# An order's book-keeping learns of twelve stores and 36 loads that GpSimd issues

## The chip, the cores and the metric

The kernel runs on one core of one Trainium2 chip. The metric is the device time of one execution in microseconds (us). Engine names: TensorE (PE, matmuls), VectorE (DVE), ScalarE (ACT), GpSimd (POOL) and SyncE (SP). DMAs are issued by instructions of SyncE, of ScalarE or of GpSimd; each of these engines takes its instructions in the order in which they were written.

## The reference, cut to what matters

```python
x = A_u                                   # 1 x 2048 x 576, f32
xn = layernorm(x)
# S4D: a long convolution per channel, 576 channels, 128 complex poles each
A = -exp(log_A_real) + 1j * A_imag;  C = (C_real + 1j * C_imag) * dt[:, None]
P = exp((A * dt[:, None])[:, :, None] * arange(2048))
K = 2 * einsum("dn,dnl->dl", C, P).real
s = irfft(rfft(xn, 4096) * rfft(K, 4096))[:2048] + xn * D_skip
# channel MLP, 576 -> 4608 -> 576
h = gelu(layernorm(xn) @ w1 + b1)
g = silu(h @ w2 + b2)
out = x + s * g
```

## The kernel before, in words

The MLP is the bulk. Tokens are held in two blocks of 512 at a time, hidden channels in twelve groups of three blocks of 128. One pair of a group and a token block is a slot; there are 48, and each has three positions of the first layer (`layer1`, 14 matmuls each, L546) and eight of the second (L638, L630, in a few slots L608). Values are split into a high and a low part, so a product takes three matmuls. After a block of the first layer ScalarE computes the gelu (L578) and its high part `hh` (L581), VectorE the low part `hl` (L584), and the second layer reads both. Weights come by SyncE and are split by ScalarE (L530) and VectorE (L527).

Between the positions lies the convolution. The channels are worked in 36 tables of 16 and six chunks of 96. A table takes the poles' parameters of its channels from `par_s` in HBM (`load_par`, L882, GpSimd's queue, two buffers `par`), computes phases (L900, L903, VectorE), folds and sines (L906 to L919, ScalarE) and magnitudes `mg` (L925), weighs them (`U`, `v`, L936 to L942), and TensorE sums over the poles (`kgen`, L982). A chunk transforms input and kernel (L1054, L1093), multiplies, transforms back (L1146, L1178); ScalarE then copies the result out of PSUM into two scratch tiles, one of `pr` and one of `ys` (L1186, two copies), and GpSimd's queue stores each with four DMAs into `s_s` in HBM (L1189). Near the end `combine_load` (L707) and `last_s` (L733) read `s_s` again, for the products with the gate and the output.

Other things on GpSimd's queue: the first layernorms (L414), reordering of constants (L288 to L310), half of `place_rest` (L664, eight small DMAs between SBUF tiles, the other half on SyncE), stores of gates (L685) and of half of the output (L719).

All of this is put into one fixed order by a planner, the class `Order`, while the program is written out. It keeps a clock for each engine. Work is held in lines of steps; a step names an engine, a duration, marks of other steps that it needs, and a mark of its own. A step with an engine starts at the later of its needs and the engine's free time and moves that engine's clock on by its duration; its result counts 0.2 us later (`LAT`). A step without an engine (`None`) writes its instructions as soon as its needs are there and gives its mark the duration later; it moves no engine's clock. Of the steps that can start by TensorE's present time, the one with the earliest start is written first; between equal starts the line that stands earlier in `od.lines` goes first. Urgent chains (gelu, `hl`, additions into `acc`, `place_rest`) have dates by which they must be done, and a line's step that would run past the next such date on its engine is put off.

So the planner's durations decide only the order in which each engine gets its instructions. On the device each instruction waits for its semaphores and for those ahead of it on its engine. In the kernel before, `load_par` is a step without an engine, and the stores L1189 are written inside the ScalarE step that copies (`store`); the planner's clock of GpSimd knows of neither. `place_rest`'s half on GpSimd is a step of 5.2 us.

Of the kernel before, what the change touches and what calls it, by code (L numbers as in the profile page):

```python
# [22 lines left out]
CH = 96  # L23
NCH = D // CH
# [9 lines left out]
PK = 72  # L34
# [9 lines left out]
def dve(n):  # L44
    return 0.075 + 0.00104 * n


def act(n):
    return 0.06 + 0.00098 * n
# [159 lines left out]
def step(eng, dur, fn, need=(), mark=None, cv=0, at=0.0, late=0.0, tbl=None, by=1e9):  # L209
    return dict(eng=eng, dur=dur, fn=fn, need=tuple(need), mark=mark, cv=cv, at=at, late=late, tbl=tbl, by=by)  # L210
# [3 lines left out]
def mixer_kernel(ctx, tc, u, log_a_real, a_imag, c_real, c_imag, log_dt, d_skip, w1, b1, w2, b2,  # L214
# [662 lines left out]
    def load_par(b):  # L877
        if b == NB:
            return
        PAR[b] = sb.tile([P, SB, NPAR], F32, name="par", bufs=2)  # L880

        nc.gpsimd.dma_start(PAR[b].rearrange("p (g i) k -> p g (i k)", g=4), dram(  # L882
            par_s, (b // 6 * CH + b % 6 * 4) * NPAR, [[D * NPAR, P], [24 * NPAR, 4], [1, 4 * NPAR]]))
# [7 lines left out]
    def tables(b):  # L891

        T = {}

        def phase(k):
            if k == 0:
                T["w"] = sb.tile([P, 2, SB, NV], F32, name="w", bufs=2)
                nc.vector.tensor_mul(T["w"][:, 1], bc(PAR[b][:, :, 0], 2, NV), bc(tv, 1, SB))  # L900
            else:
                u = T["w"][:, 1, :, 32:]
                nc.vector.tensor_add(u, u, bc(PAR[b][:, :, 1], 2, 32))  # L903

        def whole():
            nc.scalar.activation(T["w"][:, 0].bitcast(I32), T["w"][:, 1], AF.Copy)  # L906

        def frac():
            nc.vector.tensor_sub(T["w"][:, 1], T["w"][:, 1], T["w"][:, 0].bitcast(I32))

        def fold():
            nc.scalar.activation(T["w"][:, 0], T["w"][:, 1], AF.Abs)

        def sin(k):
            w = T["w"][:, k]
            if k == 0:
                nc.scalar.activation(w, w, AF.Sin, bias=halfpi[:, 0:1], scale=-TWO_PI)
            else:
                nc.scalar.activation(w, w, AF.Sin, scale=TWO_PI)  # L919

        def mags(k):
            if k == 0:
                T["m"] = sb.tile([P, SB, NM], F32, name="mg")
            n, e1, e8 = ((8, E1, E8), (4, E32, E256))[k]
            nc.vector.tensor_mul(T["m"][:, :, 64 * k:64 * k + 8 * n].rearrange("p c (i j) -> p c i j", i=n),  # L925
                                 bc(PAR[b][:, :, e8:e8 + n], 3, 8), bc(PAR[b][:, :, e1:e1 + 8], 2, n))

        def weigh(k, part):

            if part == 0:  # L930
                T["v"] = sb.tile([P, 2, SB, 64], F32, name="v")
                T["U"] = sb.tile([P, 2, SB, 32], F32, name="U")
                TAB[b] = (T["U"], T["v"])
            w, v, m = T["w"], T["v"], T["m"]
            if part == 0:
                nc.vector.tensor_mul(T["U"], w[:, :, :, 32:], bc(m[:, :, 64:], 1, 2))  # L936
            elif part == 1:
                nc.vector.tensor_mul(v[:, :, :, :32], w[:, :, :, :32], bc(m[:, :, :32], 1, 2))
            elif k == 0:
                nc.vector.tensor_mul(v[:, k, :, 32:], w[:, k, :, 31::-1], m[:, :, 32:64])  # L940
            else:
                nc.vector.scalar_tensor_tensor(v[:, k, :, 32:], w[:, k, :, 31::-1], -1.0, m[:, :, 32:64],  # L942
                                               op0=OP.mult, op1=OP.mult)

        n = SB * 32
        f = lambda g, *a: lambda: g(*a)
        return ([step(None, 6.0 if b < 3 else 4.5, lambda: load_par(b), mark=("par", b), need=[("pack", ((b // 6 + 1) * CH - 1) // PK)]
                      + ([("mags", b - 2)] if b > 1 else [("xn", k) for k in range(8, NT)])),
                 step("DVE", dve(SB * NV), f(phase, 0), need=[("wu", b - 2, 1)] if b > 1 else []),
                 step("DVE", dve(n), f(phase, 1)), step("ACT", act(SB * NV), whole),  # L950
                 step("DVE", dve(SB * NV), frac), step("ACT", act(SB * NV), fold, mark=("fold", b))],
                [step("ACT", act(SB * NV), f(sin, 0), need=[("fold", b)], mark=("sin", b, 0), tbl="sin"),
                 step("ACT", act(SB * NV), f(sin, 1), mark=("sin", b, 1), tbl="sin")],
                [step("DVE", dve(2 * n), f(mags, 0), need=[("par", b)]),
                 step("DVE", dve(n), f(mags, 1), mark=("mags", b))]
                + [step("DVE", dve(2 * n) if part < 2 else dve(n), f(weigh, k, part),
                        need=[("sin", b, int(part < 2))] + ([("kg", b - 1)] if b else []),
                        mark=("wu", b, 1) if k else None) for k, part in ((0, 0), (0, 1), (0, 2), (1, 2))])
# [55 lines left out]
    def chunk(c):  # L1014

        XC, MAT, YS = {}, {}, {}
        one, two, three = [], [], []
        line = [one]
        add = lambda *a, **k: line[0].append(step(*a, **k))

# [144 lines left out]
        def i1():  # L1165
            Q = []

            def mm():
                for f in range(2):
                    q = bank2("cv")  # L1170
                    Q.append(q[:, :, :4 * CH].rearrange("p t (i r d) -> p t i r d", i=2, r=2))
                lead(q)
                for t in range(2):
                    for e in range(4):
                        for f in range(2):
                            r = slice(64 * f, 64 * f + 64)
                            k = 4 * e + 2 * t
                            nc.tensor.matmul(Q[f][32 * e:32 * e + 32, t], g1t[r],  # L1178
                                             A2[r, k:k + 2, 1].rearrange("p i d r -> p i r d"),
                                             start=True, stop=True, skip_group_check=True)  # L1180
            add("PE", I1, mm, cv=2, mark=("i1", c))

            def store(f):
                sc = ys_tile().rearrange("p i a b d -> p i (a b) d") if f else (
                    sb.tile([P, 2, 4 * CH], F32, name="pr").rearrange("p t (i d) -> p t i d", i=4))
                nc.scalar.activation(sc, Q[f].rearrange("p t i r d -> p t (i r) d"), AF.Copy)  # L1186
                for e in (1, 3, 0, 2):
                    y, h = divmod(e, 2)
                    nc.gpsimd.dma_start(s_s[64 * y + 32 * f:64 * y + 32 * f + 32, 8 * h:8 * h + 8, c * CH:(c + 1) * CH],  # L1189
                                        sc[32 * e:32 * e + 32].rearrange("p t i d -> p (t i) d"))  # L1190
            for f in range(2):
                add("ACT", act(8 * CH), lambda f=f: store(f), cv=-1, mark=("st", c) if f else None)

        for g in range(4):
            for f in range(2):
                add(None, 4.5 if g == 3 and f == 1 else 1.0, lambda g=g, f=f: load(g, f),
                    need=() if g or f else [("xn", b) for b in range(NT)] + [("pack", D // PK - 1)])
# [15 lines left out]
    od = Order(tc, nc)  # L1213
    od.pinned = True
    el, wl2, wl, nl2, pl, pl2, pl3, pl4, pl5, nl, ml, ml2, xl, wx, c3, c2, c1, kl, tl, sl, vl, gl, fl, f2l = [od.line() for _ in range(24)]
    nlh, mlh, yl, pl6 = od.line(), od.line(), od.line(), od.line()
    od.lines = od.lines[-4:] + od.lines[:-4]
    el2 = od.line()


# [273 lines left out]
    for k in range(4):  # L1494
        gl["steps"].append(step("POOL", 5.0, lambda k=k: part.update({k: load_g2(k)}), mark=("g2", k),
                                need=[("g2c", k - 1)] if k else []))
# [24 lines left out]
    def end_line():  # L1521
        for c, c0, c1, sets in ((NCH - 3, 0, CE, [(b, 1) for b in range(8)]), (NCH - 2, CE, CL, [(0, 4), (4, 4)])):
            for b, n in sets:
                a = (b, n, c0, c1)
                ml["steps"].append(step(None, 8.0 if b else 12.0, lambda a=a: combine_load(*a), need=[("st", c), ("u", NT - 1)]))
                ml["steps"].append(step("DVE", 2 * dve(n * (c1 - c0)), lambda a=a: (gated(*a), summed(*a))))
                ml["steps"].append(step(None, 4.0, lambda: None))
        a = (0, 8, CL, D)
        ml["steps"].append(step(None, 1.0, lambda: combine_load(*a, 0), need=[("k1", NCH - 1, 1), ("x1", NCH - 1)]))
        ml["steps"].append(step(None, 16.0, lambda: combine_load(*a, 1), need=[("st", NCH - 1)]))  # L1530
        ml["steps"].append(step("DVE", dve(8 * CH) + 0.1, lambda: gated(*a)))
        ml["steps"].append(step("DVE", dve(8 * CH) + 0.1, lambda: summed(*a)))

# [36 lines left out]
    later(mid - 4, G - 1, lambda: x_free(0))  # L1570
    later(mid - 1, G - 1, lambda: x_free(1))
    later(NSLOT - 10, 4, end_line)
    sl["steps"].append(step(None, 14.0, last_s, need=[("st", NCH - 1)], mark="s8"))
    for k in range(8):
        c3["steps"].append(step(None, 5.0 if k == 0 else 2.0, lambda k=k: last_x(k), need=[("i1", NCH - 1), ("u", NT - 1)], mark=("x8", k)))

# [198 lines left out]
```

## Time and profile before

| what | us |
|---|---|
| median of 3 runs | 1071.47 (1070.90 to 1071.89) |
| profiled execution, its own time | 1071.01 |
| its span in the profile | 1069.2 |
| TensorE busy | 1058.5 (99%) |
| VectorE busy | 936.8 (88%) |
| ScalarE busy | 683.0 (64%) |
| GpSimd busy | 228.4 (21%) |

A row of the timeline reads: start, us, engine, line, operation, output tile <- input tiles, count, and in brackets the idle time of the engine before it with what released it. A row of waits reads: engine, tile and line, what it waited for, us in total, times, the longest. A row of stretches gives busy us and instruction counts of TensorE, its weight loads, VectorE, ScalarE and GpSimd, then the granted TensorE clock (1.00 is full), the DMA engines' share and GB/s. A row of groups gives us in total and mean ns of one, then the idle time before the group and what ended it. A DMA issue of GpSimd counts as busy time while GpSimd issues it; the landing is listed apart.

### The profile page before, as it was taken

Reading aid. Unit: us, or ns where it says so; the run is one execution under the profiler, and the core shown is the slowest. Engines: PE = TensorE matmul, PEld = TensorE weight load, DVE = VectorE, ACT = ScalarE, POOL = GpSimd, SP = SyncE. Lnnn points to the kernel's source line nnn. Section 1 sums busy time; section 2 is a strip of 40 time slices with the busy share of each in tenths; the row PEclk is TensorE's granted clock in tenths of the full one; section 3 lists DMA queues with packets and bytes.
Section 4 is the critical chain, followed back from the end, with each engine's and each line's share of the span. In section 5 each row is a group of like instructions: output and inputs, shape, how many; then the busy total and the mean of one; then the engine's idle time right before and its main releaser. Section 6 shows DMA issues by size and latency. Waiting matters only on the chain.

```text
span 1069.2 us, 23544 instructions
## 1 busy us (share of the span) xinstructions
PE 1058.5 (99%) x9515; PEld 874.5 (82%) x9515; DVE 936.8 (88%) x1550; ACT 683.0 (64%) x1061; POOL 228.4 (21%) x328
## 2 busy tenths in 40 slices
PE   9999999999999999999999999999999999999997
PEld 7888888888878886888877888878887888778886
DVE  7698768899899897999988989999999999867766
ACT  6658639786755766757686666856785757524344
POOL 5668533201000003002120000200002022242130
PEclk9999999999999999999999999999999999999999
DMA  7785436663213243356422215222421346365146
GB/s 232 239 267 181 123 130 226 231 158 118 92 39 101 50 85 97 98 142 162 92 69 61 92 48 115 67 79 64 106 90 50 122 122 147 101 196 155 48 119 186
DMA packets 145470, 130.93 MB, mean 122 GB/s; under 512 B 94925, under 2 KB 117233, under 8 KB 144337
## 3 DMA queue, kind: packets, MB, share of 16 engines
q1 hardware_dynamic: 127696, 78.77, 27.0%
q0 software_dynamic: 16912, 49.68, 15.0%
q8 instruction: 75, 1.23, 0.5%
q10 hardware_dynamic: 752, 0.97, 0.3%
q14 instruction: 35, 0.28, 0.1%
HBM read 98.90 MB, written 35.19 MB: 125 GB/s over the span
## 4 chain that ended last, share of the span: by engine, by line
PE 95%; DVE 2%; DMA 1%; POOL 1%; issue 1%; ACT 0%; SPq 0%; ACTq 0%; DVEq 0%; POOLq 0%
PE m L546 42%; PE m L638 30%; PE m L630 8%; PE cv L1093 3%; PE cv L982 3%; PE m L608 3%; PE cv L1054 2%; PE cv L1146 2%; PE cv L1178 1%; PE m L561 1%; DMA acc<-in_A_u_dram 0%; PE cv L608 0%; POOL s_s L1189 0%; POOL acc L664 0%; DMA row<-y_s 0%
## 5 line engine op out<-in xcount | busy, mean ns | idle before, releaser
L638 PE MATMUL m<-w2s,hh 128*128 128x448 f32 x1056 | 303.8, 369 | 0.7 <-DVE acc L643 0.6
L578 ACT ACTIVATE h<-m,b1t 128x512 f32<-128x512 f32 x144 | 99.2, 689 | 203.7 <-PE m L546 200.0
L638 PEld LDWEIGHTS m<-w2s,hh 128*128 128x128 f32 x1056 | 194.0, 188 | 36.8 <-issue 12.4
L638 PE MATMUL m<-w2s,hl 128*128 128x448 f32 x528 | 192.0, 364 | 1.8 <-DVE hl L584 1.8
L546 PE MATMUL m<-XH,w1h 128*128 128x512 f32 x564 | 155.2, 397 | 0.0
L546 PE MATMUL m<-XL,w1h 128*128 128x512 f32 x564 | 151.4, 390 | 0.0
L546 PE MATMUL m<-XH,w1l 128*128 128x512 f32 x564 | 151.0, 389 | 0.0
L584 DVE TENSOR_TENSOR hl<-h,hh 128x512 fp32r<-128x512 f32 x144 | 99.8, 694 | 50.6 <-ACT hh L581 50.0
L546 PEld LDWEIGHTS m<-XH,w1h 128*128 128x128 f32 x564 | 103.4, 188 | 30.6 <-issue 5.5
L882 POOL DMA_DIRECT2D par<-par_s x36 | 27.5, 764 | 469.3 <-DVE mg L925 436.7
L546 PEld LDWEIGHTS m<-XL,w1h 128*128 128x128 f32 x564 | 105.9, 188 | 23.0
L546 PEld LDWEIGHTS m<-XH,w1l 128*128 128x128 f32 x564 | 105.9, 188 | 22.5
L643 DVE TENSOR_TENSOR acc<-m,acc 128x448 f32<-128x448 f32 x160 | 98.1, 613 | 22.6 <-PE m L638 21.8
L638 PEld LDWEIGHTS m<-w2s,hl 128*128 128x128 f32 x528 | 99.1, 188 | 9.2 <-DVE hl L584 2.2
L581 ACT ACTIVATE hh<-h 128x512 fp32r<-128x512 f32 x144 | 90.7, 630 | 3.4
L630 PE MATMUL m<-hh,w2s 128*128 128x512 f32 x264 | 90.2, 396 | 0.0
L530 ACT ACTIVATE w2s<-raw 128x576 fp32r<-128x576 f32 (+3 forms) x75 | 46.3, 675 | 36.9 <-PE m L638 35.3
L925 DVE TENSOR_TENSOR mg<-par 128x1024 f32<-128x1024 f32 x72 | 68.0, 951 | 0.8
L630 PEld LDWEIGHTS m<-hh,w2s 128*128 128x128 f32 x264 | 50.3, 190 | 9.9
L527 DVE TENSOR_TENSOR w1l<-raw,w1h 128x384 fp32r<-128x384 f32 x98 | 49.8, 555 | 9.7 <-ACT w1h L530 9.6
L906 ACT ACTIVATE w<-w 128x1024 int32<-128x1024 f32 x36 | 37.9, 1054 | 28.8 <-DVE w L903 28.6
L546 PE MATMUL m<-XR,w1r 128*128 128x512 f32 x141 | 54.8, 389 | 0.0
(229 smaller groups left out, 1901.2 us busy)
## 6 DMA issues: line engine op xcount, KB each, us to landing
raw<-in_B_w_dram SPq DMA_DIRECT2D x75, 288.0 KB, 3.4
raw<-in_B_w_dram SPq DMA_DIRECT2D x100, 192.0 KB, 3.0
par_s<-A POOLq DMA_DIRECT2D x8, 1080.0 KB, 5.6
par<-par_s POOLq DMA_DIRECT2D x36, 240.0 KB, 3.2
f2t<-f2q SPq DMA_DIRECT2D x24, 256.0 KB, 3.7
raw<-in_B_w_dram SPq DMA_DIRECT2D x50, 96.0 KB, 3.4
u_s<-in_A_u_dram POOLq DMA_DIRECT2D x16, 288.0 KB, 4.2
xc<-xn_s SPq DMA_DIRECT2D x48, 96.0 KB, 3.7
```

The lines of the kernel that those rows point to most:

```text
L527: low_on.tensor_sub(lo, r[:m], h[:m].bitcast(F32))
L530: nc.scalar.activation(h, r, AF.Copy)
L546: nc.tensor.matmul(q, a, b, start=j == 0, stop=j == len(ops) - 1)
L578: nc.scalar.activation(t, q, AF.Gelu_apprx_tanh, bias=b1t[:, g * G + i:g * G + i + 1], scale=1.0)
L581: LAST[0] = nc.scalar.activation(hh[:, i], t, AF.Copy)
L584: nc.vector.tensor_sub(hl[:, i], t, hh[:, i].bitcast(F32))
L608: nc.tensor.matmul(q[:, :288], a[:, i, j * P:j * P + P], b[:, i, dh * 288:dh * 288 + 288], skip_group_check=alone, start=i == 0 and k == 0 ...
L630: nc.tensor.matmul(q, a[:, i], b[:, i], start=first and i == 0 and k == 0, stop=slot in CONV and i == G - 1 and k == 2, skip_group_check=True)
L638: nc.tensor.matmul(q[:, :DA], a[:, i, key * P:key * P + P], b[:, i], start=i == 0 and k == 0, stop=i == G - 1 and k == 2)
L643: nc.vector.tensor_add(o, Q2.pop(key)[:, :DA], bias2[:, :DA] if first else o)
L906: nc.scalar.activation(T["w"][:, 0].bitcast(I32), T["w"][:, 1], AF.Copy)
L925: nc.vector.tensor_mul(T["m"][:, :, 64 * k:64 * k + 8 * n].rearrange("p c (i j) -> p c i j", i=n), bc(PAR[b][:, :, e8:e8 + n], 3, 8), bc(P ...
```

## The change

The load of a table's parameters becomes a step of GpSimd of 0.8 us, and a step without an engine behind it stands for the rest of the transfer (5.2 us for the first three tables, 3.7 after; 6.0 and 4.5 in one before). The four DMAs that store a scratch tile leave the copy's step and become a step of GpSimd of their own, 2.4 us, in a new line `zl` that stands behind nearly all others; it needs the copy, and the mark `("st", c)`, on which the reads of `s_s` depend, is now that of the second store's step. The two steps that stand for the last chunk's reads of `s_s` are shortened by 5 us. No instruction is added or removed; what changes is when the planner writes them, and through its clock of GpSimd and its marks the order of the rest.

```diff
-        return ([step(None, 6.0 if b < 3 else 4.5, lambda: load_par(b), mark=("par", b), need=[("pack", ((b // 6 + 1) * CH - 1) // PK)]
+        return ([step("POOL", 0.8, lambda: load_par(b), need=[("pack", ((b // 6 + 1) * CH - 1) // PK)]
                       + ([("mags", b - 2)] if b > 1 else [("xn", k) for k in range(8, NT)])),
+                 step(None, 5.2 if b < 3 else 3.7, lambda: None, mark=("par", b)),
...
+        send_line = zl["steps"]
...
                 nc.scalar.activation(sc, Q[f].rearrange("p t i r d -> p t (i r) d"), AF.Copy)
+                SC[f] = sc
+
+            def send(f):
                 for e in (1, 3, 0, 2):
                     y, h = divmod(e, 2)
                     nc.gpsimd.dma_start(s_s[64 * y + 32 * f:64 * y + 32 * f + 32, 8 * h:8 * h + 8, c * CH:(c + 1) * CH],
-                                        sc[32 * e:32 * e + 32].rearrange("p t i d -> p (t i) d"))
+                                        SC[f][32 * e:32 * e + 32].rearrange("p t i d -> p (t i) d"))
+            SC = {}
             for f in range(2):
-                add("ACT", act(8 * CH), lambda f=f: store(f), cv=-1, mark=("st", c) if f else None)
+                add("ACT", act(8 * CH), lambda f=f: store(f), cv=-1, mark=("sc", c, f))
+                send_line.append(step("POOL", 2.4, lambda f=f: send(f), need=[("sc", c, f)], mark=("st", c) if f else None))
...
+    zl = od.line()
     el2 = od.line()
...
-        ml["steps"].append(step(None, 16.0, lambda: combine_load(*a, 1), need=[("st", NCH - 1)]))
+        ml["steps"].append(step(None, 11.0, lambda: combine_load(*a, 1), need=[("st", NCH - 1)]))
...
-    sl["steps"].append(step(None, 14.0, last_s, need=[("st", NCH - 1)], mark="s8"))
+    sl["steps"].append(step(None, 9.0, last_s, need=[("st", NCH - 1)], mark="s8"))
```

## The prediction

> **What bounds the kernel now.** I read the page first, then a table of equal stretches, then the waits of TensorE, and last the timelines of the one stretch that differs. The page's first rows say that TensorE works all the time:
>
> ```profile
> span 1069.2 us, 23544 instructions
> PE 1058.5 (99%) x9515; PEld 874.5 (82%) x9515; DVE 936.8 (88%) x1550; ACT 683.0 (64%) x1061; POOL 228.4 (21%) x328
> ...
> DVE  7698768899899897999988989999999999867766
> ```
>
> The change removes no matmul, so only TensorE's lost time can be won: 1069.2 − 1058.5 = 10.7 us of idle time, and time at a lower clock. The table in stretches of 27 us (columns: busy us and instructions of TensorE, its weight loads, VectorE, ScalarE, GpSimd; then granted clock, DMA share, GB/s) has one bad row between the start and the last 16 us:
>
> ```profile
> 378.00:405.00 27.00, 27.00 (x271) 21.58 (x277) 26.34 (x40) 18.86 (x28) 4.66 (x8) 1.00 0.35 86
> 405.00:432.00 27.00, 24.63 (x199) 18.58 (x184) 20.82 (x36) 16.51 (x23) 6.63 (x12) 0.94 0.26 71
> 432.00:459.00 27.00, 27.00 (x278) 23.14 (x277) 25.56 (x48) 20.89 (x35) 2.94 (x5) 1.00 0.49 135
> ```
>
> In 405 to 432 TensorE idles 27.00 − 24.63 = 2.37 us, the clock falls, and VectorE, busy 95 to 98% on either side, is over 5 us short. The waits of TensorE, whole span, name the same place:
>
> ```profile
> PE m L638 <- DVE hl L584: 1.8, 1, 1.8
> PE m L1241 <- POOL XL L1232: 1.3, 1, 1.3
> PE cv L432 <- DVE row L405: 0.6, 1, 0.6
> PE m L638 <- DVE acc L643: 0.6, 1, 0.6
> ```
>
> The second and third lie in the first microseconds, which the planner does not order. So before the tail there is one stall, and the first and fourth row are its two halves. Its cause stands in the timelines of GpSimd and VectorE:
>
> ```profile
> 401.09 2.33 POOL L1189 DMA_DIRECT2D s_s<-pr  x4 [16.64 <-ACT pr L1186]
> 403.42 4.38 POOL L664 DMA_DIRECT2D acc<-bias  x8
> 407.79 2.32 POOL L1189 DMA_DIRECT2D s_s<-ys  x4
> 411.31 0.77 POOL L882 DMA_DIRECT2D par<-par_s  x1 [1.19 <-issue]
> ```
> ```profile
> 398.21 0.68 DVE L925 TENSOR_TENSOR mg<-par 128x512 f32<-128x512 f32 x1
> ...
> 407.80 0.65 DVE L584 TENSOR_TENSOR hl<-h,hh 128x512 fp32r<-128x512 f32 x1
> 414.48 1.22 DVE L900 TENSOR_TENSOR w<-par,tv 128x1024 f32<-128x1024 f32 x1 [6.03 <-DMA par<-par_s]
> 415.73 0.69 DVE L903 TENSOR_TENSOR w<-w,par 128x512 f32<-128x512 f32 x1
> 416.34 0.68 DVE L584 TENSOR_TENSOR hl<-h,hh 128x512 fp32r<-128x512 f32 x1
> ```
>
> The next poles' buffer is free when `mg` is read, at 398.89. Their load (L882) goes out at 411.31, because two stores of the convolution's results (L1189) and GpSimd's half of `place_rest` (L664) stand ahead of it. VectorE takes its instructions in order: it sits 6.03 us before L900, and the hidden block's low half (`hl`, L584), which TensorE needs, stands behind L900 and L903. The planner charged GpSimd for none of the eight stores and not for the load, so it believed the parameters there and put L900 first.
>
> **What the stall costs.**
>
> ```profile
> 417.10:421.00 3.90, 3.90 (x10) 3.11 (x11) 3.90 (x7) 3.90 (x10) 0.76 (x1) 0.56 0.21 63
> ```
>
> This is the stretch right after the gap: clock 0.56 over 3.90 us, so 3.90 × 0.44 = 1.72 us lost. Sum: 2.37 idle + 1.72 clock = 4.1 us. Lower bound 2.4, were the slow clock no consequence of the gap; upper bound 4.4, if some 0.3 us of restart at the two halves is added as an estimate.
>
> Here a rule of the Trainium skill says otherwise. "TensorE: Matmul & The Clock Gate", in the part on the HAM clock gate, has the array fall to half clock after at least one idle window of about 3.4 us. The gap before the slow stretch is 1.8 us by the wait row, half of that, and yet the clock halves right behind it; the trace therefore does not agree as far as the length goes. By the page's length the slow clock would not be the gap's doing, and the sum would be 2.4 us; by the rows it is 4.1 us. I take the rows.
>
> **The change, part by part.**
>
> (1) The load of the parameters becomes a step of GpSimd of 0.8 us, then 5.2 or 3.7 us of landing. What GpSimd executes stays: 36 loads of 764 ns each.
>
> ```profile
> L882 POOL DMA_DIRECT2D par<-par_s x36 | 27.5, 764 | 469.3 <-DVE mg L925 436.7 <-DVE U L936 31.4 <-issue 1.2
> ...
> L1189 POOL DMA_DIRECT2D s_s<-pr x24 | 14.0, 592 | 68.2 <-ACT pr L1186 68.2
> ...
> L707 POOL DMA_DIRECT2D row<-s_s x10 | 5.8, 581 | 0.0
> ```
>
> In the plan each table gets its parameters 0.2 us later (0.8 + the lag of 0.2 + 5.2 against 6.0), plus what GpSimd is booked. Over 36 tables that is at most 36 × 0.2 = 7.2 us, at least nothing, where the table waits for VectorE's gaps anyway. I take nothing: VectorE is 95% full around the stall, so its gaps pace the tables, and the 6 us that it gets back point the other way.
>
> (2) The stores become steps of GpSimd of 2.4 us each, four DMAs of 0.592 = 2.37 us by its row: the booking is right. On the device 12 × 2.37 = 28 us of GpSimd are moved, not added; GpSimd is 21% busy. Moved past are GpSimd's own queue (`place_rest`, the loads, later the combine's transfers), and nothing on SP's. In the stall's place the order comes out as follows.
>
> ```profile
> 394.23 0.70 DVE L655 STREAM_TRANSPOSE bias<-acc 128x512 f32<-128x512 f32 x1
> ...
> 400.00 0.81 ACT L1186 ACTIVATE pr<-cv 128x768 f32<-128x768 f32 x1
> 400.69 0.82 ACT L1186 ACTIVATE ys<-cv 128x768 f32<-128x768 f32 x1
> 401.38 1.07 ACT L912 ACTIVATE w<-w 128x1024 f32<-128x1024 f32 x1
> ```
>
> Now the first store is issued with its ScalarE copy, `place_rest` was planned between the two copies, and the load follows the table's `fold` (L912). With the change a store can start only a copy and a lag (0.81 + 0.2 = 1.0 us) after its copy began, so `place_rest` is planned ahead of both stores. It books GpSimd for 5.2 us; `fold` is over 2.5 us after the copies began (402.45 − 400.00), so the load is ready within that booking, and in a tie at GpSimd's free time the tables' line stands before the new line, which is added late. Order: `place_rest`, load, store, store.
>
> ```profile
> par<-par_s POOLq DMA_DIRECT2D x36, 240.0 KB, 3.2
> ```
> ```profile
> DVE w L900 <- DMA par<-par_s: 7.2, 2, 6.0
> ```
>
> On the device `place_rest` has its data at 394.23 + 0.70 = 394.93 and needs 4.38 us, so the load goes at about 399.4 and lands 3.15 us later (the first row, of the DMA list, its last number): 402.6, six microseconds before VectorE reaches L900 at 407.80 + 0.65 = 408.45. Should `place_rest` still follow a store, the plan knows at least that the parameters come late, and puts `hl` ahead of L900. Either way the wait goes, and what is late next on VectorE is nothing I can see: its waits for this load are two (the second row: 7.2 us in all, the longest 6.0), and the other, 1.2 us, holds no matmul.
>
> The cover of the moved stores: ten of the combine's reads of `s_s` never waited (the row of L707, idle 0.0); only for the last chunk is there no slack, and there the queue of GpSimd holds no load of a table ahead of the stores. The scratch tiles `pr` and `ys` are written next by the products of the following chunk, behind its first transforms. Cost nothing; if a load that waits for `mg` came to stand before a store, the store waits with it, to be felt in the last chunk alone, where no load is left.
>
> (3) The durations of 16 and 14 become 11 and 9. The mark comes later: first copy's end + 0.2 + 2.4 + 2.4 + 0.2 = 5.2 us against 0.81 + 0.2 = 1.0 us, so the ends are planned 14.2 against 15.0 us after it, 0.8 us earlier. Nothing on the device is shortened. The tail:
>
> ```profile
> 1029.31 1.62 PE L1178 MATMUL cv<-A,g1t 64*32 64x384 f32 x32
> ...
> 1045.84 0.75 DVE L764 TENSOR_TENSOR w<-w,acc 128x576 f32<-128x576 f32 x1
> ...
> 1045.84:1065.14 19.30, 17.29 (x106) 15.68 (x104) 15.71 (x24) 9.94 (x20) 1.38 (x2) 1.00 0.68 187
> ```
>
> From L764 to the end VectorE has 19.30 − 15.71 = 3.6 us free, and after TensorE's last matmul comes the same chain of gate, sum and store. Term: 0, between −0.8 and +0.8.
>
> (4) All orders after the first table shift a little, since the planner decides by times. Not shown by any row; I bound it by the trace: below by −0.8 us (a seam less here and there), above by one more stall like this one, +4.1. I take 0, by the nearest row: in 48 slots this planner left one such stall, and that one came from what it did not book.
>
> **Sum.** −4.1 + 0 + 0 + 0 = −4.1 us. The profiled execution took 1071.01 us (span 1069.2 and 1.8 around it), 0.46 below the median of 1071.47. So its successor has a span of 1065.1 and a time of 1066.9, and against the median 1071.5 − 4.1 = 1067.4 us. The measurement tells some 0.2% apart, 2.1 us.
>
> **The rivals.** *A new stall takes the old one's place.* VectorE's slices stand at 8 and 9 tenths from the 17th to the 34th (the 16th, at 7, is the stall), and another order can again put a table's operation before an `hl` whose time has come. For it: the fullness. Against: no other stall in the rest of the plan. Price one stall, 4.1: 1071.5, no change.
>
> *The change does not reach the stall*: the load still goes behind everything and the plan still counts it early. Against it: the booking matches the rows. 1071.5.
>
> *The slow clock stays without the gap*: the idle time alone goes, 1071.5 − 2.4 = 1069.1. Against it: it begins at the end of the gap. (The clock gate's length in the Trainium skill's "TensorE: Matmul & The Clock Gate" would make this case.)
>
> *The last chunk slips (slower).* If the later parameters do add up (up to 7.2 us) and the last convolution step (L1178 at 1029.31) misses its place between two blocks of matmuls and goes a slot later (1058.5 / 48 = 22.1 us), `s_s` comes that much later into the tail, which has 3.6 us of VectorE's gaps to take it up. Beyond that each microsecond is one of the time: 1067.4 + 22.1 − 3.6 = 1085.9. It eats up the gain from a slip of 3.6 + 4.1 = 7.7 us on. Against it: the 6 us that VectorE gets back lie ahead of it.
>
> **How the numbers follow.** The forecast 0.58 (own range 1066.2 to 1068.6); a new stall 0.18; no reach 0.07; the slow clock stays 0.04; the last chunk slips 0.07; several new stalls, 1074 and more, 0.06. Faster: 0.58 + 0.04 = 0.62. Same: 0.18 + 0.07 = 0.25. Slower: 0.13. The range leaves the last two cases out above and a little below: from 1066.0 (4.4 and a seam) to 1072.6 (a new stall slightly dearer than the old one).
>
> **What would show it.** Right: the rows of TensorE's waits on L638 gone, granted clock 1.00 in every stretch from 27 us to the tail, L882 after L664 and ahead of both L1189 near 400 us, no wait of 6 us before L900. Step 3 right: L764 near 1045.84 less 4.1. Wrong: another TensorE wait of over 1 us for `hl`, `acc` or a weight split, a stretch with a clock under 1.00, L1178 of the last chunk beyond its block, or VectorE waiting for `s_s` in the tail.

## The result, and the profile after

| | median us | runs from to | profiled execution | its span |
|---|---|---|---|---|
| before | 1071.30 | 1070.90 to 1071.89 | 1071.01 | 1069.2 |
| after | 1065.53 | 1065.36 to 1066.03 | 1065.62 | 1063.8 |

The ratio is 0.9947 (0.9929 to 0.9964): 5.8 us faster, where 4.1 were forecast. The time lies 0.5 us under the lower end of the range. Run again beside other kernels, the changed kernel took 1065.36 us against 1071.48, ratio 0.9939 (0.9925 to 0.9954).

The page of after: TensorE is as full as before, and its clock row shows no slice below 9.

```profile
span 1063.8 us, 23536 instructions
PE 1056.2 (99%) x9515; PEld 874.9 (82%) x9515; DVE 937.8 (88%) x1550; ACT 682.4 (64%) x1061; POOL 230.7 (22%) x328
...
PEclk9999999999999999999999999999999999999999
```

The same three stretches, and the waits of TensorE, all of them:

```profile
378.00:405.00 27.00, 27.00 (x266) 21.84 (x264) 26.37 (x39) 18.89 (x28) 9.20 (x16) 1.00 0.40 100
405.00:432.00 27.00, 27.00 (x255) 20.91 (x257) 25.00 (x41) 19.27 (x27) 2.04 (x4) 1.00 0.33 95
432.00:459.00 27.00, 27.00 (x312) 22.93 (x300) 24.91 (x48) 20.97 (x36) 2.94 (x5) 1.00 0.40 103
```
```profile
PE m L1249 <- POOL XL L1240: 1.3, 1, 1.3
PE m L638 <- DVE acc L643: 0.4, 1, 0.4
PE m L561 <- ACT XH L436: 0.2, 1, 0.2
```

In 405 to 432 TensorE is busy 27.00 of 27.00 at clock 1.00, where it idled 2.37 us at 0.94, and VectorE went from 20.82 to 25.00 busy. The waits on `hl` are gone. The timelines of GpSimd and VectorE give the reason (the stores are L1194 now):

```profile
395.78 4.34 POOL L664 DMA_DIRECT2D acc<-bias  x8 [10.77 <-DVE bias L655]
400.12 0.76 POOL L882 DMA_DIRECT2D par<-par_s  x1
401.64 2.32 POOL L1194 DMA_DIRECT2D s_s<-pr  x4 [0.77 <-ACT pr L1188]
403.95 1.16 POOL L1194 DMA_DIRECT2D s_s<-ys  x2
406.28 1.16 POOL L1194 DMA_DIRECT2D s_s<-ys  x2 [1.17 <-issue]
```
```profile
408.37 0.65 DVE L584 TENSOR_TENSOR hl<-h,hh 128x512 fp32r<-128x512 f32 x1
...
410.99 0.69 DVE L584 TENSOR_TENSOR hl<-h,hh 128x512 fp32r<-128x512 f32 x1 [1.38 <-ACT hh L581]
411.60 1.22 DVE L900 TENSOR_TENSOR w<-par,tv 128x1024 f32<-128x1024 f32 x1
412.86 0.69 DVE L903 TENSOR_TENSOR w<-w,par 128x512 f32<-128x512 f32 x1
...
414.43 0.69 DVE L584 TENSOR_TENSOR hl<-h,hh 128x512 fp32r<-128x512 f32 x1
```

Two things differ from before. The load goes out at 400.12, ahead of all eight stores, not at 411.31. And VectorE's order has `hl` ahead of L900, not behind L903. The experiments below ask which of the two is worth what.

Where the time went, by the starts of the same matmuls in the profiled executions (from each trace, us; "step" runs from the first matmul of slot 19's third `layer1` block to the first of slot 20; "slots 20 to 28" from there to the first of slot 28, with the same number of matmuls of each kind before and after):

| | start of slot 0 | to slot 19's third block | step | slots 20 to 28 | on to the last matmul | behind it | span |
|---|---|---|---|---|---|---|---|
| before | 12.65 | 396.22 | 20.04 | 178.68 | 455.54 | 6.10 | 1069.23 |
| after | 13.14 | 396.26 | 15.55 | 177.91 | 455.35 | 5.62 | 1063.84 |
| after less before | +0.49 | +0.04 | −4.49 | −0.77 | −0.19 | −0.48 | −5.39 |

The first and last differences are of the single executions: some 5.6 us behind the last matmul are found in nearly every kernel below, the unchanged one in two more executions included (5.71, 5.64). The step and slots 20 to 28 are the change's. In those two executions of the unchanged kernel the step took 20.69 and 20.24, and slots 20 to 28 took 178.81 and 178.93. With the means of the three profiles of before, 20.32 and 178.81, the change won 4.77 + 0.90 = 5.7 us, near the 5.8 of the medians.

### The profile page after: what moved, and what is told of

Its sections match the earlier page's. It is cut to its first block, busy times and chain, and to the rows that moved or that the text cites. A ratio compares the mean times of both kernels' runs of the same rounds, so it can differ in the third digit from the quotient of the medians.

```text
span 1063.8 us, 23536 instructions
## 1 busy us (share of the span) xinstructions
PE 1056.2 (99%) x9515; PEld 874.9 (82%) x9515; DVE 937.8 (88%) x1550; ACT 682.4 (64%) x1061; POOL 230.7 (22%) x328
## 4 chain that ended last, share of the span: by engine, by line
PE 95%; DVE 4%; issue 1%; ACT 0%; POOL 0%; ACTq 0%; DVEq 0%; POOLq 0%
PE m L546 41%; PE m L638 29%; PE m L630 8%; PE cv L983 3%; PE cv L1095 3%; PE m L608 3%; PE cv L1056 2%; PE cv L1148 2%; PE cv L1180 1%; PE m L1249 1%; PE m L561 1%; DVE acc L643 0%; PE cv L608 0%; DVE pr L1116 0%; DVE hl L584 0%
## 5 line engine op out<-in xcount | busy, mean ns | idle before, releaser
L912 ACT ACTIVATE w<-w 128x1024 f32<-128x1024 f32 x36 | 38.1, 1058 | 27.0 <-DVE w L909 27.0
```

## The experiments

**The load on another queue, all orders as before.** The plan is untouched, so each computing engine gets its instructions in the order of before; only the stores and `place_rest` no longer stand ahead of the load.

```diff
-        nc.gpsimd.dma_start(PAR[b]..., dram(
+        nc.sync.dma_start(PAR[b]..., dram(
```

> The kernel before, but the 36 loads of the poles' parameters are issued by SyncE instead of GpSimd; the planner still counts neither them nor the stores, and the orders of TensorE, VectorE and ScalarE stay instruction for instruction those of before. Theory 'one stall': the load at the stall no longer stands behind stores and place_rest, VectorE waits for no parameters there, and the whole 4.5 us of the stall (idle, half clock and restart) go: 1066.8 us. Rival 'the new order as a whole': nothing of the order changes here, so 1071.3 us.

Measured: 1079.54 us, ratio 1.0071 (1.0055 to 1.0086), slower by 7.8. The step at the stall went to 15.55, exactly that of after, and slots 20 to 28 took 178.91, as before. But another stall came in slot 10. SyncE's queue and VectorE, from their timelines, then TensorE's longest wait, the one load's time to landing, and the stretch:

```profile
206.16 4.90 SPq L475 DMA_DIRECT2D raw<-in_B_w_dram  x4
211.10 1.25 SPq L478 DMA_DIRECT2D raw<-in_B_w_dram  x2
212.38 0.63 SPq L882 DMA_DIRECT2D par<-par_s  x1
```
```profile
225.05 1.22 DVE L900 TENSOR_TENSOR w<-par,tv 128x1024 f32<-128x1024 f32 x1 [12.21 <-DMA par<-par_s]
226.31 0.69 DVE L903 TENSOR_TENSOR w<-w,par 128x512 f32<-128x512 f32 x1
226.92 0.68 DVE L584 TENSOR_TENSOR hl<-h,hh 128x512 fp32r<-128x512 f32 x1
```
```profile
PE m L630 <- DVE hl L584: 11.1, 2, 10.9
```
```profile
DMA to landing us min/median/max: 12.6/12.6/12.6
```
```profile
206.00:225.00 19.00, 10.72 (x48) 8.63 (x46) 4.72 (x7) 8.85 (x11) 7.50 (x13) 0.86 1.01 346
```

In before this load went out on GpSimd's queue:

```profile
205.98 0.77 POOL L882 DMA_DIRECT2D par<-par_s  x1
```

It landed 7.6 us later there, at 213.55, and L900 waited 1.2 us. Now six loads of raw weights stand ahead of it; it is issued 6.4 us later, and lands 12.6 us after that, with the DMA engines full (1.01). It is the old stall in a larger size: VectorE sits 12.21 us before L900, `hl` stands behind it, and TensorE waits 10.9 us. The cause of the first stall is thereby shown (taking the load out from behind the stores ends it, with VectorE's order unchanged), and the time that I expected missed, because I did not read what stands on SyncE's queue at each of the 36 loads.

**The stores alone as steps** (the load stays a step without an engine; durations 11 and 9 as in the change).

> Only the stores become steps of GpSimd (with the durations 11 and 9); the load stays a step without an engine. At the stall GpSimd's order is that of after (place_rest, load, store, store), VectorE's is that of before (L900 ahead of hl). Theory 'the place in the queue suffices': parameters land at about 403, no wait at L900, 1066 to 1067 us. Rival 'the plan must know that the load is late': VectorE's order has not changed, the stall stays, 1071 us.

Measured: 1068.03 us (1066.15 to 1069.01), ratio 0.9962 (0.9947 to 0.9977). GpSimd's queue is that of after, VectorE's order that of before (L900 ahead of `hl`):

```profile
397.47 4.34 POOL L664 DMA_DIRECT2D acc<-bias  x8 [10.80 <-DVE bias L655]
401.80 0.76 POOL L882 DMA_DIRECT2D par<-par_s  x1
```

The step is 15.55: the place in the queue alone ends the stall. Slots 20 to 28 took 178.98, as before. This profile also loses 1.9 us near 80 us, at a wait that neither profile of the first table has:

```profile
DVE xc L801 <- DMA pr<-in_A_C_real_dram: 1.9, 1, 1.9
```

That is the landing of an early load; the wait was 0.3 us with the load on SyncE's queue, and 0.8 in one more kernel below. So single executions differ there by up to 2 us, and I read the step, not the whole time.

**The load alone as a step** (the stores stay inside the copies, durations 16 and 14).

> Only the load becomes a step of GpSimd; stores inside the copy's step, durations 16 and 14 as before. At the stall GpSimd's order is that of before (store, place_rest, store, load), VectorE's is that of after (hl ahead of L900). Theory 'the place in the queue': VectorE still waits some 6 us before L900, and what stands behind it (weight splits, the third hl) is late, so a stall of 1 to 4 us is left: 1068 to 1071 us. Rival 'the plan's knowledge suffices': the hl is ahead, TensorE waits for nothing, 1066 to 1067 us although VectorE still sits 6 us.

Measured: 1068.82 us (1067.47 to 1069.02), ratio 0.9970 (0.9958 to 0.9981). Now GpSimd's queue is that of before (the load at 412.68, behind the stores) and VectorE's order that of after:

```profile
411.33 0.69 DVE L584 TENSOR_TENSOR hl<-h,hh 128x512 fp32r<-128x512 f32 x1 [1.40 <-ACT hh L581]
415.91 1.22 DVE L900 TENSOR_TENSOR w<-par,tv 128x1024 f32<-128x1024 f32 x1 [3.88 <-DMA par<-par_s]
417.17 0.69 DVE L903 TENSOR_TENSOR w<-w,par 128x512 f32<-128x512 f32 x1
417.78 0.55 DVE L527 TENSOR_TENSOR w1l<-raw,w1h 128x384 fp32r<-128x384 f32 x1
418.25 0.68 DVE L584 TENSOR_TENSOR hl<-h,hh 128x512 fp32r<-128x512 f32 x1
```

The step is 18.25: 1.79 of the 4.49 us won, 2.70 left, because L900 still waits (3.88 us, where some 6 were expected), and the next `hl` stands behind it. Slots 20 to 28 took 177.91, as in after.

**One table's parameters planned later.** All as before, but table 13, the one that stalls, counts its load at 8.5 us.

```diff
-step(None, 6.0 if b < 3 else 4.5, lambda: load_par(b), ...
+step(None, 6.0 if b < 3 else 8.5 if b == 13 else 4.5, lambda: load_par(b), ...
```

> The kernel before; for the one table whose load is late the planner is told 8.5 us instead of 4.5, nothing else. GpSimd's order at the stall stays that of before, VectorE's becomes that of after (hl ahead of L900). 'Place in the queue': 1068 to 1071 us, VectorE still waits about 6 us. 'The plan's knowledge suffices': 1066 to 1067.5 us.

Measured: 1068.21 us (1067.92 to 1069.80), ratio 0.9969 (0.9956 to 0.9982). The queue is as before, `hl` is ahead of L900, L900 waits 3.0 us (about 6 were expected), the step is 17.38 (1.83 left), slots 20 to 28 took 177.91. With before and after these three kernels fill a square: the place in the queue alone wins the whole 4.49 of the step, the plan's knowledge alone 1.8 to 2.7 of it; the 0.8 to 1.0 us in slots 20 to 28 comes with the knowledge and not with the place. The change has both.

**After, with the old durations 16 and 14** at the last reads of `s_s`; the changed kernel ran beside it.

> The changed kernel again, beside the next ones on one chip. The stall near 414 us gone, 5 to 6 us below before (ratio 0.995); in the stretch 76 to 84 us TensorE idles between 0 and 1.2 us, as it did in executions of kernels whose order is the same up to there.

> The changed kernel with the two durations of the last reads of s_s back at 16 and 14. Theory 'the durations do nothing on the device': as the changed kernel within 1 us. Rival 'the shorter durations bring the tail forward': some 0.5 to 0.8 us longer than the changed kernel, all of it behind TensorE's last matmul.

```diff
-ml ... step(None, 11.0, lambda: combine_load(*a, 1), need=[("st", NCH - 1)])
+ml ... step(None, 16.0, lambda: combine_load(*a, 1), need=[("st", NCH - 1)])
-sl ... step(None, 9.0, last_s, need=[("st", NCH - 1)], mark="s8")
+sl ... step(None, 14.0, last_s, need=[("st", NCH - 1)], mark="s8")
```

Measured: 1065.36 us for after; 1067.72 (1067.11 to 1068.24) with the old durations, ratio to before 0.9962 (0.9948 to 0.9976). TensorE's last matmul ends at 1058.20 against 1058.06; behind it lie 7.75 us against 5.66, so nearly all of the 2.4 us, three times what the rival had named. VectorE's tail, of the old durations first, then of after:

```profile
1044.23 0.75 DVE L764 TENSOR_TENSOR w<-w,acc 128x576 f32<-128x576 f32 x1
...
1053.91 0.75 DVE L764 TENSOR_TENSOR w<-w,acc 128x576 f32<-128x576 f32 x1
```
```profile
1053.00:1065.90 12.90, 5.20 (x40) 4.97 (x38) 8.32 (x14) 2.25 (x6) 0.53 (x1) 0.88 0.74 192
```
```profile
1040.92 0.75 DVE L764 TENSOR_TENSOR w<-w,acc 128x576 f32<-128x576 f32 x1
```
```profile
1053.00:1063.80 10.80, 5.22 (x40) 4.99 (x38) 5.62 (x10) 2.25 (x6) 0.00 (x0) 0.92 0.54 134
```

With the old durations the first product with the gate starts 3.3 us later, 8.32 us of VectorE's work are left at 1053 instead of 5.62, and they end the kernel. The theory that these two edits do nothing fell; they pay for the later mark (with the old mark and the old durations, in the kernel with the load alone, 5.62 us lie behind the last matmul). Without them the mark of the change costs 2.4 us of the 5.8.

**The raw parameters' loads 6 us earlier** in the changed kernel, to see whether the spread among runs comes from their landing near 77 us (the wait at L801 of the profiles above).

```diff
- ... at=t ... for k, t in ((0, 44.0), (2, 56.0), (3, 60.0), (1, 66.0))]
+ ... at=t ... for k, t in ((0, 44.0), (2, 50.0), (3, 54.0), (1, 60.0))]
```

> The changed kernel with three of the four early loads of the raw parameters 6 us earlier in the plan (50, 54 and 60 instead of 56, 60 and 66). Theory 'the spread among runs comes from these loads landing late near 77 us': no wait of VectorE for them at L801, TensorE busy throughout 76 to 84 us, median up to 1 us below the changed kernel and a smaller spread. Rival 'the spread is elsewhere': same median and spread.

Measured: 1065.62 us (1064.99 to 1066.35), ratio 0.9942 (0.9927 to 0.9957), against 1065.36 (1065.08 to 1065.67) for after beside it. The median did not fall and the spread is not smaller. Neither profile has the wait at L801, and in both TensorE is busy throughout 76 to 84 us, so what these loads do to the spread stays open.

**What a gap does to the clock.** Two more executions of the unchanged kernel, and two kernels that repeat the third `hl` of chosen slots in after, with the same values, so that TensorE gets gaps of many lengths (the second of them repeats every other time only half of the tile).

```diff
-            nc.vector.tensor_sub(hl[:, i], t, hh[:, i].bitcast(F32))
+            for _ in range(1 + (EXTRA.get(slot0, 0) if i == 2 else 0)):
+                nc.vector.tensor_sub(hl[:, i], t, hh[:, i].bitcast(F32))
...
```

> The changed kernel with the third hl of eleven slots computed 3 to 8 times over (the same values), so that TensorE waits for VectorE some 0.6 us longer per repetition less about 0.5 us of slack: gaps of about 0.7, 1.3, 1.9, 2.5, 3.1 and 3.7 us. Theory 'a gap of under two microseconds already brings the half clock': granted clock near 0.5 for some 3 us behind the gaps of 1.8 us and more, not behind those of about 1.2 us and less. Rival 'only a whole idle window of about 3.4 us does' (the Trainium skill, 'TensorE: Matmul & The Clock Gate', on the clock gate): clock 1.00 behind all gaps but the longest.

> The changed kernel with extra repetitions of the third hl in twelve slots, sized for gaps of about 1.6 and 1.9 us, falling anywhere in the windows. Theory 'a window of 3.41 us idle for more than about half of it halves the clock in the next one': half clock only where one window holds over about 1.7 us of the gap; a gap that two windows share leaves the clock at 1.00. Rival 'the length of the gap decides': the same gap always does the same.

> The kernel before, profiled once more. If the half clock behind the stall depends on how its gap of 1.8 us falls into fixed windows of 3.41 us, this execution may show the gap with the clock at 1.00 behind it, and then the stall costs about 2.7 us instead of 4.5; if the gap alone decides, the half clock is there again.

> The kernel before, a third profile: as the second, to see whether the cost of the stall differs between executions of one program.

One execution each: 1096.51 and 1100.18 us with the gaps, 1071.05 and 1070.77 for the unchanged kernel. In all these traces the clock changes only on a fixed grid of 3.413 us. Stretches cut on that grid, in order: before at its stall; the unchanged kernel's second further execution at its stall; then three gaps of the kernels with repeats.

```profile
413.93:417.34 3.41, 1.60 (x14) 1.12 (x7) 2.83 (x4) 0.88 (x1) 0.00 (x0) 1.00 0.02 5
417.34:420.75 3.41, 3.41 (x9) 2.68 (x9) 3.41 (x7) 3.41 (x9) 0.76 (x1) 0.50 0.24 72
```
```profile
413.34:416.75 3.41, 1.99 (x21) 0.98 (x21) 1.99 (x3) 0.04 (x1) 0.00 (x0) 1.00 0.15 50
416.75:420.16 3.41, 2.37 (x9) 1.44 (x9) 3.41 (x6) 3.41 (x7) 0.76 (x1) 1.00 0.16 25
```
```profile
594.41:597.82 3.41, 1.96 (x9) 1.31 (x7) 3.30 (x5) 3.38 (x4) 0.00 (x0) 1.00 0.00 0
597.82:601.24 3.42, 1.89 (x9) 1.72 (x10) 3.32 (x6) 0.58 (x2) 0.00 (x0) 1.00 0.00 0
601.24:604.65 3.41, 3.41 (x46) 2.94 (x48) 3.13 (x5) 1.34 (x2) 0.75 (x1) 1.00 0.18 33
```
```profile
231.29:234.70 3.41, 1.69 (x8) 1.09 (x7) 3.27 (x6) 2.13 (x2) 0.00 (x0) 1.00 0.35 123
234.70:238.11 3.41, 3.41 (x19) 3.15 (x18) 2.48 (x6) 2.76 (x3) 0.95 (x2) 1.00 0.00 0
...
398.54:401.95 3.41, 1.56 (x8) 1.12 (x7) 3.38 (x8) 0.47 (x2) 0.00 (x0) 1.00 1.04 223
401.95:405.36 3.41, 3.41 (x11) 3.00 (x11) 3.08 (x6) 2.42 (x3) 0.00 (x0) 0.50 0.92 146
```

An idle time of 3.41 − 1.60 = 1.81 us within one stretch halves the whole next one. In the second pair the gap was longer, 2.0 us, but the grid cut it into 1.42 and 0.57 (the rest of the second stretch's idle time are later, shorter waits): no halving. A gap of 2.98 us, cut into 1.45 and 1.53, left the clock whole too. 1.72 in one stretch did not halve it, 1.85 did. Over all gaps of these five traces between the first 30 us and the tail, idle times of 1.81 to 2.67 us in one stretch were followed by half clock (ten times, in one of them from a stretch that was already slow), 1.72 and less, in a stretch at full clock, never. So neither of the rivals holds: no stretch had to be idle as a whole, and the length of the gap alone does not decide. About half of one stretch idle fits them all.

And yet the stall cost 4.49 us with a half clock (20.04 against 15.55), 5.14 with one (20.69), and 4.69 without (20.24). What it did follow is VectorE. "Third `hl`" is its start after slot 19's third `layer1` block began:

| kernel | third `hl` | later than after | step | longer than after | difference | clock |
|---|---|---|---|---|---|---|
| after | 5.03 | | 15.55 | | | 1.00 |
| one table later | 7.62 | 2.59 | 17.38 | 1.83 | 0.76 | 1.00 |
| load alone | 8.50 | 3.47 | 18.25 | 2.70 | 0.77 | 1.00 |
| before | 10.29 | 5.26 | 20.04 | 4.49 | 0.77 | one stretch 0.50 |
| before, third execution | 10.48 | 5.45 | 20.24 | 4.69 | 0.76 | 1.00 |
| before, second execution | 10.92 | 5.89 | 20.69 | 5.14 | 0.75 | one stretch 0.50 |

TensorE lost what VectorE was late, less 0.76 us of slack, to within 0.02 us, with the half clock or without. The slow stretch fills time in which TensorE would have waited again: within the step it idles 2.37 and 3.01 us in the two executions with the half clock, and 3.58 us in the one without.

## Why the prediction was wrong, point by point

**Where the stall is and what makes it: right.** The load behind the stores, L900 in front of `hl`: moving the load alone ended the stall with VectorE's order unchanged, and planning alone shortened it.

**(2), the order on GpSimd: right to the instruction.** `place_rest`, load, store, store; the load at 400.12 where about 399.4 was worked out. L900 follows `hl` without a wait. (The table's `fold` ends 2.45 us after the copies began, not "over 2.5"; nothing hangs on it.) What the prediction took for one mechanism is two: it said that either way the wait goes, and with the planning alone 3.88 us of it stayed.

**The stall's price: a step that failed, by its size, some 0.4 to 0.7 of the 1.9 us.** The sum "2.37 idle + 1.72 clock = 4.1" had an upper bound of 4.4; the runs show 4.49 in the same execution and 4.77 as a mean of three. Adding the two was the wrong sum, and no row or run shows the 0.3 us of restart that its upper bound added. The slow stretch hid inside VectorE's lateness, and a second execution's stall cost as much with the clock whole. What should have been read is VectorE: 6.03 us idle before L900, less the time that it would have waited for `hh` anyway (after shows 1.38), is about 4.65 to be won. The exact account is the table's: the third `hl` 5.26 us earlier, less 0.76 of slack, gives the 4.5.

The rule of the Trainium skill on the clock gate ("TensorE: Matmul & The Clock Gate", What's actually happening) would have left 2.4 us, and fell as a rival: there is no slow clock in after, nor in its second profile. But the argument that I set against it was also wrong. The clock did halve behind a gap of about half the page's window, as I said; it did not carry the price.

**(4), the other orders: the other step that failed, and the larger part: taken as 0, measured −0.8 to −1.0.** The 0 was reasoned for new stalls alone; that another order can make eight slots shorter entered only as the bound of −0.8, which was about right but stood on no row, and the sum took nothing of it. Of the gain in slots 20 to 28, up to 0.45 us is a wait of TensorE on `acc` near 472 us that two of the three profiles of before have and after has not (in the third execution 178.93 us long, 178.48 busy); the rest is the same number of matmuls put together in another sequence, and why that sequence is shorter stays open. It came wherever the plan knew that table 13's parameters are late, and not in the two kernels that keep TensorE's order of before (the load on SyncE's queue 178.91, the stores alone 178.98). Together, 4.77 − 4.1 and 0.9 make 1.6 of the 1.9 us between 1067.4 and 1065.53 (the median of before, 0.2 lower beside the changed kernel, is most of the rest) and put the time under the range, which had room for 4.4 and a seam of 0.8 only.

**(1), 0.2 us at each table: right.** Up to slot 19's third block the two kernels differ by 0.04 us.

**(3), the durations: right in the sum, wrong in the reason.** L764 came at 1040.92, where 1045.84 less 4.1 is 1041.74: it moved with TensorE. But the term of 0 is two halves: the later mark with the old durations costs 2.4 us, and the shorter durations give them back, and the bound of ±0.8 for it would not have held either half.

**The rivals.** No new stall: the longest new wait of TensorE is 0.4 us. The last chunk did not slip by a slot; with the old durations it cost 2.4 us, the same mechanism in small.

## What to carry to other kernels

If a planner writes a fixed order, every DMA issue that shares a queue has to be on that queue's clock. A load that it believes to be there is worse than one it knows to be late, since the waiting instruction holds up all that stands behind it on its engine. This stall was priced, in the five executions that had it, by the lateness of the engine that paces the work behind it, less the slack there, and not by adding up the idle time and the slow clock of the engine that shows it. When a mark moves, the durations that hang on it have to be set again, and moving a transfer to a queue that looks free asks for that queue's traffic at every one of its places (12.2 us of waiting at one of 36 here).

## What the runs showed of the hardware

The granted clock changed only on a grid of 3.413 us, and the grid lay differently to the work in each execution. One stretch with 1.81 us or more of TensorE idle was followed by a whole stretch at 0.50; 1.72 us was not, nor was a gap of 2.98 us that the grid cut in two. Coming back is another matter: with the load on SyncE's queue a stretch already at half clock that held 1.06 us of idle was followed by one more at half. The Trainium skill, "TensorE: Matmul & The Clock Gate" (What's actually happening), gives the same window, 3413 ns, and calls it free-running: the traces agree. The same section names at least one idle window as the condition. Here 1.81 us of idle in one, about half of it, was enough, so a gap's length alone does not tell whether the clock falls.
